# A chooser that also scores the last visit, and the denominators' step given out one visit sooner

## The chip, the cores and the metric

The kernel runs on one core of a Trainium2 chip. A core has five engines that run side by side and wait for each other through semaphores: PE (TensorE, matrix products into PSUM), DVE (VectorE), ACT (ScalarE), POOL (GpSimd) and SP (SyncE, which here issues the transfers). PSUM has eight banks; a bank holds a product until DVE or ACT has read it. The metric is the device time of one execution in microseconds (us). Before the change it is 592.06 us, the median of 3 runs (591.94 to 592.22).

## The reference

Two stages follow each other: attention through 32 induced points, for each of four images of 12480 rows of 128 channels, and a dense layer with a leaky activation.

```python
def mab(q, kv):
    s = scale * (q @ kv.transpose(0, 2, 1))
    s = s - s.max(-1, keepdims=True)
    a = np.exp(s)
    a /= a.sum(-1, keepdims=True) + 1e-09
    return a @ kv
h = mab(I, x)            # 32 induced points look at an image's rows
attn = mab(x, h)         # the rows look at the 32 results
...
h = x @ w_in             # 49920 rows, 128 -> 2048
g = np.maximum(h, 0.0) + alpha * np.minimum(h, 0.0)
out = g @ w_out          # 2048 -> 128
```

## The kernel before

**The dense layer carries the time.** The rows are worked in 98 blocks of up to four tiles of 128 rows. A block is gone through in *visits*, four for a block of four tiles and two for the very last block, which has two tiles: 390 visits, counted from 0. A visit (`visit`, L791) makes four first-stage products (L809: 128 of the 2048 features by up to 512 rows, each into a PSUM bank of its own, named `hh`) and four activations, each of which reads one bank and writes one second-stage operand, `gt`, to SBUF; ACT (L822) or DVE (L824) does each. The second stage (`second`, L827; products at L835) multiplies the four gts with the output weights and adds them in the block's PSUM bank `bp`. The leaky part is linear and is added by `linear` (L847, L862). Below, gt 156.2 is operand 2 of the operands 0 to 3 of visit 156, hh 156.2 the product it is made from; "aavv" means that ACT makes operands 0 and 1 of a visit and DVE 2 and 3.

**The order of PE** is: the products of visit n, then the second stage of visit n - 1, then the small products of the steps given out at visit n. PE works its queue in that order, so a first-stage product whose bank isn't free yet holds up the second stage behind it.

**The attention is woven in.** While one image is in the dense layer, the next image's induced points are worked out in small steps, given out at set visits with `at(n, fn, ..., cost=...)`. The steps at the end of an image's first attention, for images 1 to 3 (image 0 is done before the visits begin), are `a_max`, `a_factors`, `a_parts`, `a_den`, `a_sum` and `a_w_both`. `a_parts` (L557) joins the induced points' denominators: ACT makes the weights of the parts, `ex` (`a_worth`, L544), DVE multiplies them with the parts' sums, `ex` (`a_total`, L554), and adds these up, `den` (L555). `a_den`, two visits later, has PE turn `den` into the divisors (L568). The results are the same whenever between the last part and `a_den` this is done.

**Who does what is chosen by a model.** The class `Plan` keeps, for each of some 64 candidate plans, when PE, ACT and DVE will be free and when each bank will be. `choose` (L230) goes visit by visit: for each candidate it tries every split of the four activations, who does a block's copy out of PSUM (`finish`, L873: ACT at L888 or DVE at L890), and whether a step is done at once ("n") or held ("l"). A held step is run in the next visit, between operands 1 and 2 (`run_waiting`, called in `visit` when r is 2). `step` (L154) gives the state after the visit; its first entry is PE's time, which is nearly all of the score by which candidates are kept. The second stage that it counts in visit n is that of visit n - 1. In `step`, the parts of a step that is done at once follow each other, a DVE part starting when the ACT part is done (`busy[k] = ready = max(busy[k], ready) + ns`); a held step's parts are put on their engines one by one:

```python
if r == 2:
    for k, ns, ready, bank in late:
        busy[k] = max(busy[k], ready) + ns
```

The `ready` there is the one noted when the step was held, so a held DVE part doesn't wait in the model for the ACT part ahead of it. `plan.bank()` hands out the banks as the model chose them.

Of the kernel before, what the change touches and what calls it, by code (L numbers as in the profile page):

```python
# [30 lines left out]
def kernel(  # L31
# [80 lines left out]
    class Plan:  # L112
# [117 lines left out]
        def choose(self):  # L230
            start = tuple(430.0 if k == BANKS - 1 else 0.0 for k in range(BANKS))
            beam = [((0.0, 0.0, 330.0, (0.0,) * R, start, (), ()), None)]
            relus = ["".join(w) for w in product("av", repeat=R) if 0 < w.count("a") < R]
            for n, (*_, chains) in enumerate(self.visits):
                ways = []
                for chain in chains:
                    kinds = [k for k, _ in chain]
                    if "f" in kinds:
                        ways.append([e + w for e in "av" for w in "nl"])
                    elif "!" in kinds or not {"a", "v"} & set(kinds):  # L240
                        ways.append([""])
                    else:
                        ways.append(["n", "l"])
                found = {}
                for state, path in beam:
                    for way in product(*ways):
                        for relu in relus:
                            new, used = self.step(state, n, relu, way)
                            at = new[0] + 390
                            over = max(new[1] - at, 0) + max(new[2] - at, 0)  # L250
                            over += sum(w[1] for w in new[6]) * 0.3
                            score = new[0] + 0.3 * over
                            ends = sorted(max(x - new[0], -200) for x in new[4])
                            key = (
                                *(int(x - new[0]) // 16 for x in new[1:3] + new[3]),
                                *(int(x) // 16 for x in ends if x < self.NEVER / 2),
                                new[6],
                            )
                            if key not in found or score < found[key][0]:
                                found[key] = (score, new, (path, relu + "".join(way), used))  # L260
                best = sorted(found.values(), key=lambda f: f[0])[: self.WIDTH]
                beam = [(new, path) for _, new, path in best]
            path, taken, banks = beam[0][1], [], []
            while path:
                path, these, used = path
                taken.append(these)
                banks.append(used)
            self.taken = iter("".join(reversed(taken)))
            self.banks = iter([k for used in reversed(banks) for k in used])

    plan = Plan()
# [919 lines left out]
    visits = [(blk, i) for blk in blocks for i in range(NV // blk.per)]  # L1191
# [8 lines left out]
    def at(n, fn, *args, cost=()):  # L1200


        todo.setdefault(max(n, 0), []).append((fn, args, cost))
# [12 lines left out]
    for b, s, nt in groups[1:]:  # L1216
        n = first[b, s]
# [3 lines left out]
        if (b, s) == (0, 2):  # L1221
# [7 lines left out]
            cost=[("a", 100 + 27 * nt)],  # L1229
# [24 lines left out]
    for b in range(B - 1):  # L1254
        n = first[b, 0] - 1
        if b:
            at(n - 4, lambda b=b: states.__setitem__(b + 1, new_state(b + 1)))
        for p, pc in enumerate(whole_pieces):
            m = n + (8 * (p - 1 + (not b and p > 2)) if p > 1 else p)
            load, cast, turn = m - 3, m + 6, m + 8  # L1260
            score = m + 15 if p > 1 else n + 16
            look = score + 1 + (p == 1)
            join = m + (24 if p == whole_pieces[-1].k else 23) if p > 1 else n + (31 if p else 23)
            if not b:
                load, cast, turn = {
                    0: (-1, -1, 6), 1: (-1, 9, 10), 2: (4, 9, 11)
                }.get(p, (load, cast, turn))
                score, look = (score, look) if p > 1 else (score + 4, look + 4)
                join = n + 31 if p < 2 else n + 39 if p < 3 else join
            f = pc.full  # L1270
            if load >= 0:
                at(load, on, b + 1, a_load, pc)
            if cast >= 0:
                at(cast, on, b + 1, a_cast, pc)
            else:
                for q, v in enumerate((3, 4, 5, 5)):
                    at(v, on, b + 1, a_cast_act, pc, q * BT, BT, cost=[("a", 560)])
            at(turn, on, b + 1, a_turn, pc)
            small_at(
                score,  # L1280
                on,
                b + 1,
                a_scores_least,
                pc,
                cost=[("s", 215 if f else 85), ("v", 800 if f else 460)],
            )
            at(look, on, b + 1, a_exp, pc, cost=[("a", 717 if f else 430)])
            at(look + 2, on, b + 1, a_fac, pc, cost=[("a", 220)] if p else [])
            at(look + 1, on, b + 1, a_e1, pc)
            small_at(  # L1290
                join, on, b + 1, a_h_add, pc, cost=[("s", 226 if f else 115), ("v", 260)]
            )
        m = n + 8 * (NS - 2 + (not b)) + 15
        at(m + 2, on, b + 1, a_max, cost=[("a", 200)])
        at(m + 4, on, b + 1, a_factors, cost=[("s", 200), ("v", 170), ("a", 205)])
        at(m + 6, on, b + 1, a_parts, cost=[("a", 220), ("v", 260)])
        at(m + 8, on, b + 1, a_den, cost=[("s", 200), ("v", 370)])
        at(m + (12 if b else 10), on, b + 1, a_sum, cost=[("s", 200), ("v", 110)])
        small_at(m + 14, on, b + 1, a_w_both, cost=[("s", 220), ("a", 487)])
        small_at(m + 14, on, b + 1, a_lin, cost=[("s", 75), ("v", 190)])  # L1300
# [4 lines left out]
    for n, (blk, i) in enumerate(visits):  # L1305
        before = visits[n - 1][0] if n else None
        nt = before.nt * before.per if n else 0
        chains = [cost for _, _, cost in todo.get(n, ()) if cost]
        if i == 0 and n > NV:
            copy = ("f", 0) if n > ST else ("v", 610)  # L1310
            chains.insert(0, [("acc", before.k), copy])
            if n == 2 * NV:
                chains.insert(0, [("acc", 0), copy])
        both = [b.k for b in pairs.get(n, ())]
        cost = nt * Plan.FREE if both else 0
        plan.visits.append(
            (blk.nt * blk.per * P, cost, (both, [before.k] if n else []), nt, chains)
        )
    plan.choose()

    prev = None
# [49 lines left out]
```

## Time and profile before

| | |
|---|---|
| median of 3 runs | 592.06 us (591.94 to 592.22) |
| the profiled execution | 592.11 us, span 590.3 us |
| PE busy | 582.9 us, 99% |
| DVE busy | 535.0 us, 91% |
| ACT busy | 537.6 us, 91% |
| POOL busy | 217.1 us, 37% |
| first-stage products L809 on PE | 155.4 us, 1664 of them |
| second-stage products L835 on PE | 417.2 us, 6240 |
| activations on ACT, L822 | 455.3 us, 854 of 606 ns |
| activations on DVE, L824 | 453.7 us, 706 of 684 ns |

The span is the time from the first to the last instruction in the trace; the time of an execution has 1.8 us more around it. The page gives shares over the whole span. A line of the timeline is: start in us, length in us, engine, line of the kernel, operation, output and inputs, shapes, and "xN" where N such instructions follow each other (the length then runs from the first one's start to the last one's end, and instructions of one engine may overlap by a tenth of a microsecond); in brackets the idle time of the engine ahead of it and what ended that. A line of the list of waits is: the instruction that waited, what it waited for, the sum in us, how often, and the longest. A product's line on PE is its start; matrix products overlap, and the distance of two starts is what PE needs for one.

### The profile page before, as it was taken

How to read it: one execution, taken by the hardware profiler on the slowest of the kernel's cores; microseconds unless marked ns; L12 is line 12 of the kernel's file. 1: busy time of each engine (PE TensorE's matmuls, PEld its weight loads, DVE VectorE, ACT ScalarE, POOL GpSimd, SP SyncE). 2: the span in 40 equal slices, each digit the busy share in tenths (PEclk: the TensorE clock that was granted, in tenths of full speed). 3: DMA queues.
4: the chain of work that ended last, by engine and by line, in shares of the span. 5: the costliest groups of instructions: out<-in, count | busy, mean ns of one | idle time of the engine just before them, and what ended most of it. 6: DMA issues, size and time to landing. Idle time of an engine off the chain costs nothing.

```text
span 590.3 us, 23123 instructions
## 1 busy us (share of the span) xinstructions
PE 582.9 (99%) x9492; PEld 440.0 (75%) x9492; DVE 535.0 (91%) x979; ACT 537.6 (91%) x1087; POOL 217.1 (37%) x262
## 2 busy tenths in 40 slices
PE   9999999999999999999999999999999999999997
PEld 6577777777777777777777777777777777777776
DVE  5899999988998999999999899999999999999996
ACT  5799999999999999999999999999998998999986
POOL 3485552523325525413326256124034134144110
PEclk9999999999999999999999999999999999999999
DMA  8968699532188999332258899531331341433421
GB/s 336 276 181 176 158 250 197 132 98 73 39 240 159 209 216 222 94 95 58 78 152 181 194 255 204 136 100 38 92 77 50 92 81 49 118 85 57 92 69 47
DMA packets 122411, 80.56 MB, mean 136 GB/s; under 512 B 103824, under 2 KB 106176, under 8 KB 119232
## 3 DMA queue, kind: packets, MB, share of 16 engines
q1 hardware_dynamic: 122080, 78.99, 55.3%
q8 instruction: 74, 1.21, 0.8%
q14 instruction: 33, 0.27, 0.2%
q10 hardware_dynamic: 224, 0.09, 0.1%
HBM read 28.07 MB, written 25.56 MB: 91 GB/s over the span
## 4 chain that ended last, share of the span: by engine, by line
PE 95%; DMA 3%; DVE 1%; DVEq 0%; ACT 0%; issue 0%; POOL 0%; SPq 0%
PE bp L835 66%; PE hh L809 22%; DMA xs<-in_x_dram 3%; PE bp L862 2%; PE hh L645 2%; PE hh L473 1%; PE hh L379 1%; PE bp L960 0%; PE hh L364 0%; PE hh L599 0%; DVEq L1366 0%; PE hh L456 0%; DVE xn L349 0%; PE hh L583 0%; DVE hs L489 0%
## 5 line engine op out<-in xcount | busy, mean ns | idle before, releaser
L822 ACT ACTIVATE gt<-hh 128x512 bf16<-128x512 f32 x854 | 455.3, 606 | 34.4 <-PE hh L809 29.5
L824 DVE TENSOR_SCALAR gt<-hh 128x512 bf16<-128x512 f32 x706 | 453.7, 684 | 24.0 <-PE hh L809 13.6
L835 PE MATMUL bp<-W,gt 128*128 128x128 bf16 x6240 | 417.2, 220 | 0.7 <-DVE gt L824 0.7
L835 PEld LDWEIGHTS <-gt 128*128 128x128 bf16 x6240 | 349.4, 98 | 84.6 <-issue 76.0
L809 PE MATMUL hh<-a,HW 32*128 32x512 bf16 (+2 forms) x1664 | 155.4, 370 | 0.0
L759 POOL TENSOR_TENSOR rep<-e,rc 128x2048 bf16<-128x2048 f32 (+2 forms) x26 | 84.8, 3265 | 23.0 <-DVE rc L750 22.6
L727 POOL TENSOR_TENSOR e<-e,smx 128x512 f32<-128x512 f32 (+1 forms) x24 | 24.6, 1026 | 154.7 <-ACT gt L822 83.5
L809 PEld LDWEIGHTS <-HW 32*128 32x128 bf16 x1664 | 40.4, 91 | 41.6 <-issue 5.8
L713 POOL TENSOR_TENSOR t<-e 128x256 f32<-128x256 f32 (+1 forms) x24 | 17.2, 718 | 142.5 <-ACT e L689 142.5
L888 ACT COPY ob<-bp 128x512 f32<-128x512 f32 (+1 forms) x63 | 36.9, 586 | 4.5 <-PE bp L835 1.4
L713 POOL TENSOR_TENSOR t<-t 128x128 f32<-128x128 f32 (+3 forms) x100 | 30.5, 305 | 7.8
L330 POOL CAST xn<-xs 128x2048 bf16<-128x2048 f32 x17 | 32.1, 1890 | 0.8 <-DMA xs<-in_x_dram 0.3
L890 DVE COPY ob<-bp 128x512 f32<-128x512 f32 x31 | 21.3, 686 | 5.2 <-PE bp L835 5.2
L393 DVE TENSOR_SCALAR_CACHE_REDUCE s<-hh 128x512 f32<-128x512 f32 (+2 forms) x29 | 18.0, 619 | 1.6 <-PE hh L379 1.6
L862 PEld LDWEIGHTS <-a 32*128 32x128 bf16 x392 | 15.0, 93 | 5.7
L862 PE MATMUL bp<-HA,a 32*128 32x128 bf16 x392 | 19.1, 214 | 0.0
L418 ACT ACTIVATE e1T<-s,rm 128x512 bf16<-128x512 f32 (+1 forms) x25 | 18.0, 719 | 0.3
L722 DVE TENSOR_REDUCE smx<-e 128x16 f32<-128x512 f32 (+1 forms) x24 | 15.9, 662 | 0.0
L689 ACT ACTIVATE e<-e 128x512 f32<-128x512 f32 (+1 forms) x24 | 15.0, 624 | 0.0
L960 PE MATMUL bp<-blank 128*128 128x256 bf16 x78 | 13.6, 308 | 1.2 <-DVE blank L910 1.2
L489 DVE SCALAR_TENSOR_TENSOR hs<-hs,fac,hh 128x128 f32<-128x128 f32 (+1 forms) x25 | 8.6, 344 | 5.9 <-PE hh L473 5.2
L703 ACT COPY e<-hh 128x512 f32<-128x512 f32 (+1 forms) x22 | 13.4, 609 | 0.0
(107 smaller groups left out, 202.1 us busy)
## 6 DMA issues: line engine op xcount, KB each, us to landing
out_dram<-ob SPq DMA_DIRECT2D x97, 256.0 KB, 2.6
xs<-in_x_dram SPq DMA_DIRECT2D x23, 1024.0 KB, 6.1
xs<-in_x_dram SPq DMA_DIRECT2D x2, 512.0 KB, 9.2
w_in_f<-in_moe_w_in_dram SPq DMA_DIRECT2D x1, 1024.0 KB, 4.8
a<-rep SPq DMA_TRANSPOSE x27, 4.6
xT<-xn SPq DMA_TRANSPOSE x18, 5.7
e<-e1T SPq DMA_TRANSPOSE x18, 3.6
xs_left<-in_x_dram SPq DMA_DIRECT2D x4, 64.0 KB, 5.0
```

What stands on the lines that cost most here:

```text
L330: nc.gpsimd.tensor_copy(out=st.xn[s][:], in_=xs[:])
L393: nc.vector.tensor_scalar(out=s1[:parts, :cols], in0=ps[:parts, :cols], scalar1=-scale, scalar2=None, op0=MULT, op1=MIN, accum_out=st.mx[: ...
L713: nc.gpsimd.tensor_tensor(out=t[:, :n], in0=src[:, :n, :w], in1=src[:, :n, w : 2 * w], op=ADD)
L727: nc.gpsimd.tensor_tensor(out=st.e2[s][:, :n], in0=st.e2[s][:, :n], in1=st.m2[s][:, :n].unsqueeze(2).broadcast_to([P, n, M]), op=SUB,)
L759: nc.gpsimd.tensor_tensor(out=st.rep[s][:, ts], in0=st.e2[s][:, ts].unsqueeze(2).broadcast_to([P, n, R, M]), in1=rc[:, ts].unsqueeze(2).un ...
L809: nc.tensor.matmul(hh[:, q * cols + w.start : q * cols + w.stop], HWs[b][rows, v * P : (v + 1) * P], a2[rows, t0 : t0 + nt, :].rearrange(" ...
L822: nc.scalar.activation(out=gt[:, :cols], in_=hh[:, :cols], func=RELU)
L824: nc.vector.tensor_relu(gt[:, :cols], hh[:, :cols])
L835: nc.tensor.matmul(blk.acc[:, t * C : (t + 1) * C], gt[:, (q * nt + t) * P : (q * nt + t + 1) * P], W1[:, k, :], start=(not blk.begun), st ...
L862: nc.tensor.matmul(blk.acc[w, t * C : (t + 1) * C], blk.a2[rows, blk.t0 + t, w], HAs[b][rows, :], start=(not blk.begun and t == 0), stop=F ...
L888: nc.scalar.copy(out=ob[:, :nt], in_=acc)
L890: nc.vector.tensor_copy(out=ob[:, :nt], in_=acc)
```

## The change

Two edits. The chooser's score for the last visit (n = 389) is replaced: instead of PE's time with some weight on how late ACT and DVE are, it is the time at which the second stage of this visit itself would end, operand by operand, each taken when PE is free and the operand is ready. `plan.end` is the number of products that an operand takes there, 4. And `a_parts` is given out at m + 5 in place of m + 6, for each of images 1 to 3.

```diff
                             score = new[0] + 0.3 * over
+                            if n == len(self.visits) - 1:
+                                score = new[0] - self.MODE
+                                for ready in new[3]:
+                                    score = max(score, ready + self.SEM) + self.end * self.FREE
                             ends = sorted(max(x - new[0], -200) for x in new[4])
...
         at(m + 4, on, b + 1, a_factors, cost=[("s", 200), ("v", 170), ("a", 205)])
-        at(m + 6, on, b + 1, a_parts, cost=[("a", 220), ("v", 260)])
+        at(m + 5, on, b + 1, a_parts, cost=[("a", 220), ("v", 260)])
         at(m + 8, on, b + 1, a_den, cost=[("s", 200), ("v", 370)])
...
+    plan.end = visits[-1][0].nt * visits[-1][0].per
     plan.choose()
```

What becomes of it in the built program: PE, POOL and SP have the same instructions in the same order. On ACT and DVE the order differs at four places, and the rest is the same:

```
image 1, visits 68 and 69
  ACT before  gt68.0 gt68.1 gt69.0 gt69.1 [ex] gt69.3 gt70.0 gt70.1
  ACT after   gt68.0 gt68.1 [ex] [copy ob] gt69.2 gt69.3 gt70.0 gt70.1 gt70.2
  DVE before  gt67.3 gt68.2 gt68.3 [copy ob] [ex den] gt69.2 [rc] gt70.2 gt70.3
  DVE after   gt67.3 [ex den] gt68.2 gt68.3 gt69.0 gt69.1 [rc] gt70.3
image 2, visit 156 (image 3, visit 252, likewise)
  ACT both    gt156.0 gt156.1 [ex] [copy ob] gt157.2 gt157.3
  DVE before  gt155.3 gt156.2 gt156.3 [ex den] gt157.0 gt157.1
  DVE after   gt155.3 [ex den] gt156.2 gt156.3 gt157.0 gt157.1
the last two visits
  ACT before  gt388.0 gt388.1 [copy ob] gt389.2 gt389.3 [copy ob, last]
  ACT after   gt388.0 gt388.1 gt388.2 gt389.0 gt389.1 [copy ob] [copy ob, last]
  DVE before  gt388.2 gt388.3 gt389.0 gt389.1
  DVE after   gt388.3 gt389.2 gt389.3
```

For images 2 and 3 `a_parts` was done at once, in visits 156 and 252; now it is given out in visits 155 and 251 and held. For image 1 it was held before, too. In visits 70 to 192 many products get another bank number, and so does hh 389.3. These bank pairings are the same before and after: hh 157.3 is written to the bank that gt 156.2 empties, hh 253.3 to that of gt 252.2, and hh 69.2 to that of gt 68.2.

## The prediction

> **What bounds the kernel now.** I read the page first (busy shares, granted clock, chain), then the list of waits, then the timeline at the places where the order of instructions moves. Products and their operands are named as in the section on the kernel: gt 156.2 is the third of the four second-stage operands of visit 156 (counted from 0), hh 157.3 the fourth first-stage product of visit 157.
>
> ```profile
> span 590.3 us, 23123 instructions
> ...
> PE 582.9 (99%) x9492; PEld 440.0 (75%) x9492; DVE 535.0 (91%) x979; ACT 537.6 (91%) x1087; POOL 217.1 (37%) x262
> ...
> PEclk9999999999999999999999999999999999999999
> ...
> PE 95%; DMA 3%; DVE 1%; DVEq 0%; ACT 0%; issue 0%; POOL 0%; SPq 0%
> ```
>
> PE is the bound: busy 99% at full granted clock, 95% of the chain. DVE and ACT, at 91%, are close behind. So a moved DVE or ACT instruction costs nothing while PE finds its operands and its PSUM banks ready, and costs one for one as soon as it doesn't: PE has no idle time in which to catch up. The list of waits says how often that happens now:
>
> ```profile
> DVE ex L554 <- ACT ex L544: 1.0, 1, 1.0
> ...
> PE bp L835 <- DVE gt L824: 0.7, 2, 0.5
> ```
>
> PE waits for an operand twice, for 0.7 us in all, and DVE waits for ACT's `ex` once. All three belong to places that the change touches: 0.49 and 0.95 us at `a_parts` of image 1 (timeline at 132 to 133 us), 0.20 us in the very last visit (585.66).
>
> **The change, part by part.** PE, GpSimd and SP get the same instructions in the same order as before, so no product, transfer or GpSimd step is added or dropped, and no queue of those three is passed. On DVE and ACT the four activations' split differs in visits 69, 70, 388 and 389, one `ob` copy goes from DVE to ACT, and `a_parts` (ACT `ex`, then DVE `ex` and `den`) stands earlier for images 1 to 3.
>
> *Images 2 and 3.* For image 2 the DVE pair `ex`, `den` used to stand behind gt 156.3 and now stands ahead of gt 156.2. ACT's `ex` doesn't move: on its queue it follows gt 156.1 in both. The timeline of before, DVE, ACT and PE:
>
> ```profile
> 256.70 0.69 DVE L824 TENSOR_SCALAR gt<-hh 128x512 bf16<-128x512 f32 x1
> ...
> 257.66 0.30 ACT L544 ACTIVATE ex<-rm 128x7 f32<-128x7 f32 x1
> 257.75 0.40 PE L809 MATMUL hh<-a,HW 32*128 32x512 bf16 x4
> ...
> 257.99 0.17 DVE L554 TENSOR_TENSOR ex<-ex,da 128x7 f32<-128x7 f32 x1
> 258.08 1.07 PE L835 MATMUL bp<-W,gt 128*128 128x128 bf16 x16
> ...
> 258.27 0.68 DVE L824 TENSOR_SCALAR gt<-hh 128x512 bf16<-128x512 f32 x1
> ...
> 258.87 0.68 DVE L824 TENSOR_SCALAR gt<-hh 128x512 bf16<-128x512 f32 x1
> ```
>
> ACT's `ex` ends at 257.66 + 0.30 = 257.96, and DVE's `ex` already starts 0.03 us behind it. It can't start sooner after the change. So DVE stands still with both gts of visit 156 queued behind the wait, and the place at 258.27, which was gt 157.0's, becomes that of gt 156.2: it ends at 258.27 + 0.68 = 258.95 instead of 256.70 + 0.69 = 257.39.
>
> Who waits for it: hh 157.3, because in both kernels it is written to the PSUM bank that gt 156.2 empties. It was started at 257.75, with 0.36 us to spare; now it can't before 258.95 plus the time from a DVE end to PE's start. For that the trace has one row pair, in image 1 below (DVE ends at 132.31 + 0.68 = 132.99, PE goes on at 133.05: 0.06 us); I take 0.06, with ends at 0 and at 0.20 (the whole idle time of the last visit). PE's next work, the second-stage products of visit 156, starts 258.08 - 257.75 = 0.33 us behind: 258.95 + 0.06 + 0.33 = 259.34 instead of 258.08, **+1.26 us**. Nothing is added to it after that: a product takes 1.00 / 16 = 0.0625 us, so gt 156.3 (end 258.87 + 0.68 = 259.55) is wanted at 259.34 + 12 x 0.0625 = 260.09; gt 157.0 and 157.1, two steps of 0.60 us later (260.15 and 260.75), are wanted at 260.66 and 260.91. That is a margin of 0.10 us for the last, so a second wait is near. DVE is level with PE again at gt 158.1.
>
> Image 3 has the same order and the same bank pairing (hh 253.3 behind gt 252.2):
>
> ```profile
> 395.57 0.30 ACT L544 ACTIVATE ex<-rm 128x7 f32<-128x7 f32 x1
> ...
> 395.66 0.39 PE L809 MATMUL hh<-a,HW 32*128 32x512 bf16 x4
> ...
> 395.98 1.07 PE L835 MATMUL bp<-W,gt 128*128 128x128 bf16 x16
> ...
> 396.18 1.96 DVE L824 TENSOR_SCALAR gt<-hh 128x512 bf16<-128x512 f32 x3
> ```
>
> 396.18 + 0.68 + 0.06 + 0.32 = 397.24 instead of 395.98: **+1.26 us**.
>
> *Image 1.* Here the triple moves by a whole visit, from between gt 69.1 and 69.2 to between gt 68.1 and 68.2; the copy of L890 leaves DVE for ACT, and visit 69 becomes DVE, DVE, ACT, ACT.
>
> ```profile
> 129.66 1.08 ACT L822 ACTIVATE gt<-hh 128x512 bf16<-128x512 f32 x2
> 130.25 0.43 PE L809 MATMUL hh<-a,HW 32*128 32x512 bf16 x4
> 130.40 0.68 DVE L890 COPY ob<-bp 128x512 f32<-128x512 f32 x1
> 130.61 1.07 PE L835 MATMUL bp<-W,gt 128*128 128x128 bf16 x16
> ...
> 131.70 0.30 ACT L544 ACTIVATE ex<-rm 128x7 f32<-128x7 f32 x1
> ...
> 131.93 0.62 PE L835 MATMUL bp<-W,gt 128*128 128x128 bf16 x8
> 132.03 0.17 DVE L554 TENSOR_TENSOR ex<-ex,da 128x7 f32<-128x7 f32 x1 [0.95 <-ACT ex L544]
> ...
> 132.31 0.68 DVE L824 TENSOR_SCALAR gt<-hh 128x512 bf16<-128x512 f32 x1
> ...
> 133.05 0.62 PE L835 MATMUL bp<-W,gt 128*128 128x128 bf16 x8 [0.49 <-DVE gt L824]
> 133.50 0.36 PE L568 MATMUL hh<-mf,den 128*128 128x32 f32 x2
> ```
>
> Before, PE stops in the middle of visit 69's second stage: eight products from 131.93, then the ninth at 133.05 instead of 131.93 + 8 x 0.0625 = 132.43. These **0.62 us are gained back**. But a longer stop comes one visit earlier. ACT's two gts of visit 68 (129.66, 1.08 long) end at 130.74; `ex` overlaps the one ahead of it by 0.12 (130.73 + 1.09 against 131.70 in the old place) and ends near 130.92. DVE's `ex` follows at 130.95, gt 68.2 another 132.31 - 132.03 = 0.28 later at 131.23, ending at 131.91. hh 69.2 is written to the bank that gt 68.2 empties, so it starts at 131.97 and not at 130.25, and visit 68's second stage at 131.97 + 0.32 = 132.29 instead of 130.61: +1.68. Net of the old stop: **+1.06 us**. The copy on ACT lies behind this stop (its next gt waits for hh 69.2 anyway) and costs nothing; without that cover it would cost the 0.6 us of an ACT copy. `rc` of L750 comes some 0.7 us later, and the 3.6 us GpSimd product behind it has several visits until its transposed result is read: nothing.
>
> *The other banks.* From visit 70 to 192 the same tiles get other bank numbers, mostly a plain renaming. PE's first-stage products show no idle time before, so no gain is to be had; the cost is between 0 and one wait like the 0.49 above. I take 0.
>
> *The last visit.* It is scored by what its own second stage costs.
>
> ```profile
> 583.77 0.41 PE L809 MATMUL hh<-a,HW 32*128 32x64 bf16 x32
> 583.88 0.59 ACT L888 COPY ob<-bp 128x512 f32<-128x512 f32 x1 [0.34 <-PE bp L835]
> ...
> 584.12 1.34 PE L835 MATMUL bp<-W,gt 128*128 128x128 bf16 x20
> 584.31 1.29 DVE L824 TENSOR_SCALAR gt<-hh 128x512 bf16<-128x512 f32 x2 [0.43 <-PE hh L809]
> 584.36 1.09 ACT L822 ACTIVATE gt<-hh 128x512 bf16<-128x512 f32 x2
> 584.49 0.38 SPq L898 DMA_DIRECT2D out_dram<-ob  x1
> 585.66 0.84 PE L835 MATMUL bp<-W,gt 128*128 128x128 bf16 x12 [0.20 <-DVE gt L824]
> ```
>
> PE reads the operands in order 0 to 3. Before, DVE makes 0 and 1, one behind the other, and PE waits for 1 (584.31 + 1.29 = 585.60) until 585.66. After, ACT makes 0 and 1, DVE 2 and 3, and the copy is held back behind ACT's pair (its old place at 583.88 goes to the gt that ACT takes over in visit 388). ACT can start when DVE did, at 584.31; its pair, 1.09 long, ends at 585.40, so PE goes on at 585.46: **-0.20 us**. Operand 3 (DVE, 585.60) is wanted at 585.46 + 0.50. The held copy ends near 585.9, and its transfer is issued 1.4 us later than at 584.49, still ahead of the last two, which follow the copy behind PE's end. The ends of this term are -0.29 (PE without any wait: 584.12 + 20 x 0.0625 = 585.37 against 585.66) and 0 (the last transfers caught behind that one).
>
> **The sum**: 1.06 + 1.26 + 1.26 - 0.20 = **+3.38 us**. The profiled execution took 592.11 us (span 590.3 and 1.8 around it), the median is 592.06: 595.4 us from either. What a measurement of this kernel can tell from no change is about 0.2%, 1.2 us.
>
> [...] In the trace the granted clock holds through the stop of image 1:
>
> ```profile
> 131.60:133.10 1.50, 1.01 (x15) 0.61 (x14) 1.03 (x5) 1.50 (x5) 0.64 (x3) 1.00 0.46 175
> 133.10:137.10 4.00, 4.00 (x72) 3.24 (x72) 3.68 (x9) 3.09 (x7) 3.61 (x1) 1.00 0.00 0
> ```
>
> The clock column is 1.00 in and behind a stop of 0.5 us; no stop of 1.7 us is in this trace. [...]
>
> **The rivals.**
> 1. *Not slower*: gt 156.2 and its twins have enough slack that DVE's wait is hidden, image 1's stop goes, and the end is shorter: 592.06 - 0.62 - 0.20 = 591.2. For it: both of PE's old waits go, and DVE is idle for 9% of the span. Against it: the place is the bank of hh 157.3, the price 1.26 us, and it decides as soon as gt 156.2 ends later than 257.75 - 0.06; the rows put it at 258.95. 4%.
> 2. *Only images 2 and 3 pay*: in image 1 the old stop goes and the new one is hidden, since the copy has left DVE: 592.06 + 2.52 - 0.62 - 0.20 = 593.8. Against it: ACT's `ex` can't end before 130.9, whatever DVE has to do. 8%.
> 3. *Knock-on*: the 0.10 us margin at gt 157.1 (and its like in the other two images) fails, or a renumbered bank waits; a wait of 0.49 in each image: 595.4 + 1.5 = 596.9. 9%.
> 4. [...] 2%.
> 5. *The change does nothing that shows* (DVE's `ex` doesn't hold the gts): 592. Against it: the 0.95 us in image 1, where gt 69.2 stood behind exactly this wait while its product was done by 130.7. 1%.
>
> **How the numbers follow.** The forecast, 595.4, has 76%; its own range, from the ends above (three times -0.06 to +0.14, the last visit -0.09 to +0.20), is 595.1 to 596.1. Reaching to rival 2 below and most of the way to rival 3 above gives 593.7 to 596.6, which leaves out less than 2 in 10. Faster by over 0.2% needs 590.9 or less, below even rival 1: 1%. Within 0.2%: rivals 1 and 5, 5%. Slower: 94%.
>
> **What the next profile would show.** DVE `ex` L554 waiting for ACT `ex` L544 three times, some 1.3 us in images 2 and 3 and 1.8 in image 1; PE idle ahead of L809 for DVE gt, 1.2 to 1.7 us each; no wait of L835 at visit 69; the last L835 wait down to some 0.1 us or none. The prediction falls if PE shows no wait at L809 near 131.9, 258.9 and 398 us, or if waits of the same size stand anywhere else.

## The result, and the profile after

The changed kernel takes 595.89 us (median of 6 runs, 595.51 to 596.17) against 592.06 us of the kernel before (median of 6 on the same chip, 591.92 to 592.58): a ratio of 1.0062 (95% interval 1.0051 to 1.0073), 3.83 us more. 595.4 was forecast. The profiled execution took 595.51 us, 0.38 below the median, with a span of 593.7. The page of the changed kernel, first the shares and the granted clock, then the chain, then two groups of PE (busy us, mean ns, idle us just before them):

```profile
span 593.7 us, 23121 instructions
PE 584.5 (98%) x9492; PEld 440.5 (74%) x9492; DVE 533.1 (90%) x977; ACT 538.6 (91%) x1089; POOL 217.0 (37%) x262
...
PEclk9999999999999999999999999999999999999999
...
PE 93%; DMA 3%; DVE 2%; ACT 1%; issue 0%; POOL 0%; ACTq 0%; DVEq 0%; SPq 0%
...
L839 PE MATMUL bp<-W,gt 128*128 128x128 bf16 x6240 | 417.1, 220 | 0.1
...
L813 PE MATMUL hh<-a,HW 32*128 32x512 bf16 (+2 forms) x1664 | 156.9, 370 | 3.1 <-DVE gt L828 3.1
```

Line numbers are 4 higher than before (L813 is the first-stage product, L839 the second-stage one, L828 DVE's gt, L558 DVE's `ex`, L548 ACT's). The second-stage products are as busy as before (417.1 and 417.2 us). New are the 3.1 us of idle time ahead of first-stage products, all of them for a gt of DVE, and DVE's share of the chain, 2% instead of 1%. The list of waits has the cause and the effect, three times each, and has lost PE's 0.7 us at L835:

```profile
DVE ex L558 <- ACT ex L548: 4.5, 3, 1.8
...
PE hh L813 <- DVE gt L828: 3.1, 3, 1.3
```

The timeline of the changed kernel at image 2, where the prediction's arithmetic was longest:

```profile
258.84 0.30 ACT L548 ACTIVATE ex<-rm 128x7 f32<-128x7 f32 x1
258.93 0.39 PE L813 MATMUL hh<-a,HW 32*128 32x512 bf16 x3
259.03 0.59 ACT L892 COPY ob<-bp 128x512 f32<-128x512 f32 x1
259.17 0.17 DVE L558 TENSOR_TENSOR ex<-ex,da 128x7 f32<-128x7 f32 x1 [1.35 <-ACT ex L548]
...
259.45 2.47 DVE L828 TENSOR_SCALAR gt<-hh 128x512 bf16<-128x512 f32 x4
...
260.18 0.37 PE L813 MATMUL hh<-a,HW 32*128 32x512 bf16 x1 [0.86 <-DVE gt L828]
260.49 1.07 PE L839 MATMUL bp<-W,gt 128*128 128x128 bf16 x16
```

DVE stands for 1.35 us behind ACT's `ex`, which ends at 258.84 + 0.30 = 259.14. Then it makes gt 156.2, 156.3, 157.0 and 157.1 in one piece. Three of visit 157's four first-stage products start from 258.93 on, the fourth, hh 157.3, waits until 260.18, and with it the whole second stage of visit 156, which starts 1.56 us behind 258.93 instead of 0.33. So the loss is 1.23 us, though the bracket shows 0.86: an idle time is counted from the recorded end of the last product, not from where the next could have started. Image 3 is the same (DVE waits 1.35 us, PE 0.86, at 398 and 399 us).

Image 1 in the changed kernel:

```profile
130.00 0.39 PE L813 MATMUL hh<-a,HW 32*128 32x512 bf16 x2
...
130.37 0.32 ACT L548 ACTIVATE ex<-rm 128x7 f32<-128x7 f32 x1
...
130.71 0.17 DVE L558 TENSOR_TENSOR ex<-ex,da 128x7 f32<-128x7 f32 x1 [1.80 <-ACT ex L548]
...
130.99 2.47 DVE L828 TENSOR_SCALAR gt<-hh 128x512 bf16<-128x512 f32 x4
...
131.73 0.39 PE L813 MATMUL hh<-a,HW 32*128 32x512 bf16 x2 [1.33 <-DVE gt L828]
132.05 1.07 PE L839 MATMUL bp<-W,gt 128*128 128x128 bf16 x16
...
133.38 1.07 PE L839 MATMUL bp<-W,gt 128*128 128x128 bf16 x16
```

PE stops at hh 69.2 for DVE's gt 68.2, and in visit 69 the sixteen second-stage products (133.38) run in one piece where before they came eight and eight with the stop between. The end of the program:

```profile
587.75 2.17 PE L839 MATMUL bp<-W,gt 128*128 128x128 bf16 x32
587.94 1.08 ACT L826 ACTIVATE gt<-hh 128x512 bf16<-128x512 f32 x2 [0.27 <-PE hh L813]
587.95 1.29 DVE L828 TENSOR_SCALAR gt<-hh 128x512 bf16<-128x512 f32 x2 [0.99 <-PE hh L813]
588.91 0.59 ACT L892 COPY ob<-bp 128x512 f32<-128x512 f32 x1
...
589.53 0.38 SPq L902 DMA_DIRECT2D out_dram<-ob  x1
```

The last 32 products run without a stop.

**Where the time went.** The start of each visit's first product in the changed kernel, less that in the kernel before, tells where PE falls behind. It changes at six places only: by +1.68 at visit 70 and -0.67 at 71 (image 1, +1.02 net), +0.10 at visit 101 and +0.31 at 135, +1.23 at 158 (image 2), +1.23 at 254 (image 3), and -0.24 at the end. That is 1.02 + 0.40 + 1.23 + 1.23 - 0.24 = +3.64 us. The stretch ahead of the visits differs by -0.25 between these two executions; in all the profiles shown here it lies between -0.43 and +0.44 of the kernel before, whatever was changed, so it belongs to no edit. So the spans of these two executions differ by 3.4, while the medians, each over executions whose first stretch may differ likewise, differ by 3.83.

The steps at visits 101 and 135 weren't in the forecast. This is the first of them:

```profile
174.07 0.40 PE L813 MATMUL hh<-a,HW 32*128 32x512 bf16 x4
174.92 1.29 DVE L828 TENSOR_SCALAR gt<-hh 128x512 bf16<-128x512 f32 x2 [0.39 <-ACT e L693]
175.40 0.63 PE L813 MATMUL hh<-a,HW 32*128 32x512 bf16 x4
```

DVE's gt 99.0 could be made once its product is done (174.07 + some 0.4) but starts at 174.92, 0.35 us later than the like instruction of other visits, and the next visit's four first-stage products take 0.63 us instead of 0.40: the fourth of them starts at 175.66, 0.05 behind the end of gt 99.0 (175.61), which frees a bank. The release named in the bracket is only the nearest event. The second case is gt 133.0 at 224.20.

### The profile page after: what moved, and what is told of

It is laid out like the page before. It is cut to its first block, busy times and chain, and to the rows that moved or that the text cites. A ratio compares the mean times of both kernels' runs of the same rounds, so it can differ in the third digit from the quotient of the medians.

```text
span 593.7 us, 23121 instructions
## 1 busy us (share of the span) xinstructions
PE 584.5 (98%) x9492; PEld 440.5 (74%) x9492; DVE 533.1 (90%) x977; ACT 538.6 (91%) x1089; POOL 217.0 (37%) x262
## 4 chain that ended last, share of the span: by engine, by line
PE 93%; DMA 3%; DVE 2%; ACT 1%; issue 0%; POOL 0%; ACTq 0%; DVEq 0%; SPq 0%
PE bp L839 64%; PE hh L813 21%; DMA xs<-in_x_dram 3%; PE bp L866 2%; PE hh L649 2%; PE hh L477 1%; DVE gt L828 1%; PE hh L383 1%; ACT gt L826 1%; PE bp L964 0%; PE hh L368 0%; PE hh L603 0%; DVE hs L493 0%; PE hh L460 0%; DVE xn L353 0%
## 5 line engine op out<-in xcount | busy, mean ns | idle before, releaser
L828 DVE TENSOR_SCALAR gt<-hh 128x512 bf16<-128x512 f32 x705 | 452.5, 683 | 25.3 <-PE hh L813 13.9
L839 PE MATMUL bp<-W,gt 128*128 128x128 bf16 x6240 | 417.1, 220 | 0.1
L839 PEld LDWEIGHTS <-gt 128*128 128x128 bf16 x6240 | 349.3, 98 | 86.5 <-issue 78.7
L813 PE MATMUL hh<-a,HW 32*128 32x512 bf16 (+2 forms) x1664 | 156.9, 370 | 3.1 <-DVE gt L828 3.1
L731 POOL TENSOR_TENSOR e<-e,smx 128x512 f32<-128x512 f32 (+1 forms) x24 | 24.6, 1026 | 157.1 <-ACT gt L826 79.4
L813 PEld LDWEIGHTS <-HW 32*128 32x128 bf16 x1664 | 40.5, 91 | 43.2 <-issue 7.4
L892 ACT COPY ob<-bp 128x512 f32<-128x512 f32 x64 | 37.5, 586 | 3.6 <-PE bp L839 0.7
(107 smaller groups left out, 202.0 us busy)
```

The source lines that it names most:

```text
L731: nc.gpsimd.tensor_tensor(out=st.e2[s][:, :n], in0=st.e2[s][:, :n], in1=st.m2[s][:, :n].unsqueeze(2).broadcast_to([P, n, M]), op=SUB,)
L813: nc.tensor.matmul(hh[:, q * cols + w.start : q * cols + w.stop], HWs[b][rows, v * P : (v + 1) * P], a2[rows, t0 : t0 + nt, :].rearrange(" ...
L828: nc.vector.tensor_relu(gt[:, :cols], hh[:, :cols])
L839: nc.tensor.matmul(blk.acc[:, t * C : (t + 1) * C], gt[:, (q * nt + t) * P : (q * nt + t + 1) * P], W1[:, k, :], start=(not blk.begun), st ...
L892: nc.scalar.copy(out=ob[:, :nt], in_=acc)
```

## The experiments

The changed kernel makes two edits, and the second acts at three images. The theory ("queue theory" in the expectations) is the prediction's: a held `a_parts` puts DVE's `ex` ahead of two gts, it waits there for ACT's `ex`, and PE loses what the gts come late. The table gives, for each kernel, by how much PE fell behind the kernel before in stretches of visits (the differences of start times at visits 65, 80, 150, 165, 248, 262 and 389, one profile each, us), their sum, and the median less that of the kernel before on the same chip, which was 592.06 to 592.23. A positive number is time lost. What happens between the first visit and visit 65 isn't in the table; it is nothing but for +0.12 in the kernel before with one less on DVE and +0.10 in the last kernel, both taken up below:

| kernel | image 1 (65-80) | 80-150 | image 2 (150-165) | 165-248 | image 3 (248-262) | 262-389 | end | sum | median |
|---|---|---|---|---|---|---|---|---|---|
| the change | +1.02 | +0.40 | +1.23 | 0 | +1.23 | 0 | -0.24 | +3.64 | +3.83 |
| score alone | 0 | 0 | 0 | 0 | 0 | 0 | -0.19 | -0.19 | -0.22 |
| step moved, old score | +1.02 | +0.41 | +1.23 | 0 | +1.23 | 0 | +0.01 | +3.90 | +4.05 |
| moved for images 2, 3 | 0 | 0 | +1.23 | +0.28 | +1.23 | 0 | -0.25 | +2.49 | +2.11 |
| moved for image 1 | +1.02 | +0.42 | 0 | 0 | 0 | 0 | -0.25 | +1.19 | +1.16 |
| model mended | -0.48 | +0.14 | +0.02 | +0.32 | -0.26 | +0.26 | -0.21 | -0.21 | -0.22 |
| step split | -0.25 | +0.42 | 0 | 0 | 0 | 0 | -0.22 | -0.05 | -0.27 |
| model mended, m + 6 | -0.52 | 0 | 0 | 0 | 0 | +0.09 | -0.23 | -0.66 | -0.90 |
| other banks | +0.94 | +0.41 | +1.18 | -0.01 | +1.18 | 0 | -0.22 | +3.48 | +3.33 |
| one more on DVE | +1.02 | 0 | +1.23 | +0.80 | +1.23 | 0 | -0.25 | +4.03 | +3.46 |
| before, one less on DVE | 0 | +0.40 | -0.01 | 0 | -0.28 | 0 | +0.01 | +0.12 | +0.11 |
| model mended, m + 6, spares 7 and 6 | -0.54 | -0.01 | -0.01 | 0 | -0.28 | +0.26 | -0.24 | -0.83 | -0.81 |
| model mended, m + 6, spares 2 and 3 | -0.54 | +0.37 | -0.01 | 0 | -0.28 | +0.11 | -0.25 | -0.61 | -0.59 |

**Each edit alone.** First the score without the move:

```diff
-        at(m + 5, on, b + 1, a_parts, cost=[("a", 220), ("v", 260)])
+        at(m + 6, on, b + 1, a_parts, cost=[("a", 220), ("v", 260)])
```

> The new score of the last visit alone, a_parts back at m + 6. Queue theory (the cost of the change is DVE's ex and den waiting for ACT's ex with gts queued behind them): only the last two visits differ from before, the last second stage loses most of its 0.36 us wait: 592.06 - 0.24 = 591.8, and no late DVE start in visits 99 and 133. Rival (the new score costs, by a worse plan somewhere): over 592.6.

Measured: 591.93 us (591.51 to 593.75), ratio 0.9999 (0.999 to 1.0008). The end is 0.19 us shorter and no other place moves. That is too little for a median to tell; the place shows it. Then the move without the score:

```diff
-                            if n == len(self.visits) - 1:
-                                score = new[0] - self.MODE
-                                for ready in new[3]:
-                                    score = max(score, ready + self.SEM) + self.end * self.FREE
...
-    plan.end = visits[-1][0].nt * visits[-1][0].per
```

> a_parts at m + 5 alone, with the old score. Queue theory: everything of the changed kernel but the gain at the end: 595.9 + 0.24 = 596.1, three waits of DVE's ex for ACT's ex, 4.5 us in all. Rival (score and step only cost together): under 593. If the two late DVE starts (gt 99.0 and gt 133.0, about 0.35 us each) belong to the new bank numbers of visits 70 to 192, they are there again; if they are chance, not at both of these places.

Measured: 596.20 us (595.5 to 596.48), ratio 1.0061 (1.0048 to 1.0074). Every step of the whole change is there but the one at the end. So all of the loss belongs to the moved step, and the two edits don't act on each other.

**Each image alone.** Images 2 and 3:

```diff
-        at(m + 5, on, b + 1, a_parts, cost=[("a", 220), ("v", 260)])
+        at(m + (5 if b else 6), on, b + 1, a_parts, cost=[("a", 220), ("v", 260)])
```

> a_parts at m + 5 for images 2 and 3 only, m + 6 for image 1; new score. The bank numbers of visits 70 to 192 are those of before. Queue theory: 592.06 + 2 x 1.23 - 0.24 = 594.3, PE's first-stage products wait 1.25 us for DVE gt twice, the old stop of 0.66 us in visit 69 is still there. Rival (image 1 carries the loss): 592 to 593. Rival (the renumbered banks carry much of it): the same 594.3, but then the next run has over 593.5.

Measured: 594.26 us (594.0 to 594.39), ratio 1.0032 (1.002 to 1.0044). And image 1:

```diff
-        at(m + 5, on, b + 1, a_parts, cost=[("a", 220), ("v", 260)])
+        at(m + (6 if b else 5), on, b + 1, a_parts, cost=[("a", 220), ("v", 260)])
```

> a_parts at m + 5 for image 1 only; new score. Queue theory: 592.06 + 1.02 - 0.24 = 592.8, and 0.40 more, 593.2, if the late DVE starts in visits 99 and 133 come with the new bank numbers, which this kernel has too. Rival (image 1's old stop goes and the new one is hidden): 591.2.

Measured: 593.31 us (592.98 to 595.05), ratio 1.002 (1.0011 to 1.0028). The waits of the kernel with images 2 and 3 moved, then of that with image 1 moved:

```profile
DVE ex L558 <- ACT ex L548: 3.6, 3, 1.3
...
PE hh L813 <- DVE gt L828: 1.7, 2, 0.9
```

```profile
DVE ex L558 <- ACT ex L548: 1.8, 1, 1.8
...
PE hh L813 <- DVE gt L828: 1.3, 1, 1.3
```

With images 2 and 3 the three waits are those two and the old one of image 1 (3.6 us in all against 4.5). The two kernels are 2.11 and 1.16 us over the kernel before, 3.27 together. Both have the gain of 0.24 at the end, which the whole change has once, so by these medians the change should cost 3.27 + 0.24 = 3.51, 0.32 less than it does. The places are the firmer evidence: each image's step is the same alone as together. The late DVE starts come with image 1's edit and not with those of images 2 and 3.

**The same step, with a model that knows the wait.** If DVE's standing behind ACT's `ex` is the cause, a chooser that counts it should put the step elsewhere:

```diff
-                    for k, ns, ready, bank in late:
-                        busy[k] = max(busy[k], ready) + ns
+                    done = 0
+                    for k, ns, ready, bank, linked in late:
+                        ready = max(ready, done) if linked else ready
+                        busy[k] = done = max(busy[k], ready) + ns
...
-                ready, bank = 0, None
+                ready, bank, held_one = 0, None, False
...
-                        waits.append((k, ns, ready, bank))
+                        waits.append((k, ns, ready, bank, held_one))
+                        held_one = True
```

> The changed kernel with the chooser's model mended: a held step's DVE part waits for the held ACT part ahead of it. The plan then has ACT make ex ahead of its gts and DVE take gt n.0 and n.1 before ex and den, so DVE has nothing to wait for. Queue theory: the three new stops and the old one of 0.66 us are gone, the end stays shorter: 592.06 - 0.67 - 0.24 = 591.15, or 591.5 if the new bank numbers bring late DVE starts again. Rival (the place one visit sooner costs whatever the order, since two more instructions stand ahead of the gts): 594 to 595.

Measured: 592.01 us (591.56 to 592.56), ratio 0.9991 (0.9979 to 1.0004). Given out at m + 5 as in the change, the step costs nothing: image 1 gains 0.48, images 2 and 3 are where they were. By the kinds of instructions (which operand a gt makes may differ), the order of ACT and DVE is that of the changed kernel but at the three images: there ACT's `ex` stands two gts sooner and DVE's `ex` and `den` two gts later. The timeline of that kernel at image 2 shows why; ACT's `ex` is done 1.01 us before DVE comes to its own:

```profile
255.77 0.36 ACT L551 ACTIVATE ex<-rm 128x7 f32<-128x7 f32 x1
...
257.14 0.16 DVE L561 TENSOR_TENSOR ex<-ex,da 128x7 f32<-128x7 f32 x1
```

I had expected 591.15 to 591.5; what is missing went to late starts of the kind shown above at two other instructions (+0.31 at visit 204 behind gt 202.0, +0.25 at 275) and to a step of +0.14 at visit 116. That step is likely of the same kind on ACT, though no run tests it: ACT's five gts from 191.35 on take 2.69 us here and 2.56 in the kernel with the mended model at m + 6 below, and one of the five is number 576 of ACT's records, a place of the sort that the late starts turn out to have. The -0.26 at image 3 is one that the kernel before has there and this one hasn't.

**The two halves of the step a visit apart.** ACT's part at m + 5, DVE's at m + 6:

```diff
-        at(m + 5, on, b + 1, a_parts, cost=[("a", 220), ("v", 260)])
+        at(m + 5, on, b + 1, lambda st: plan.then(lambda: a_worth(st)), cost=[("a", 220)])
+        at(m + 6, on, b + 1, lambda st: plan.then(lambda: a_total(st)), cost=[("v", 260)])
```

> Only ACT's part of a_parts goes out at m + 5, DVE's part stays at m + 6; new score, model as it was. Queue theory: for images 2 and 3 the order is that of before; for image 1 ACT's ex ends near 130.9 and DVE's ex follows gt 68.3 with a wait of some 0.5 us that the slack of gt 69.0 covers, so the old stop goes: 591.2, or 591.6 with the late DVE starts in visits 99 and 133. Rival (the sooner ACT part is what costs): over 593.

Measured: 591.96 us (591.68 to 592.83), ratio 0.9998 (0.999 to 1.0007). By the kinds of instructions, ACT's order is that of the changed kernel, and DVE's differs in one thing: at each image `ex` and `den` stand two gts later. Of the three waits of DVE one of 0.5 us is left, and the list has no wait of PE's in the dense layer:

```profile
DVE gt L828 <- ACT ob L892: 0.6, 1, 0.6
...
DVE ex L558 <- ACT ex L548: 0.5, 1, 0.5
```

So it isn't the earlier visit of ACT's half that costs, but that DVE's half goes into it as well, ahead of two gts. The first of these lines is one of the late starts: they are here too, and take back 0.42 of what image 1 and the end gain. I had expected 591.6 with them. Image 1 gains only 0.25 of the 0.67: four of its first-stage products, from 131.21 on, take 0.74 us where those of the kernel before (131.61) take 0.40. What holds them up wasn't looked at.

**The mended model with the step at its old visit.** The edit above and `m + 6`:

> The mended model and the new score with a_parts at m + 6 as before. In image 1 the copy and ex change places on ACT and DVE takes gt 69.0 and 69.1 before ex. Queue theory: 592.06 - 0.67 - 0.24 = 591.15, or 591.6 with the late DVE starts. Same banks as in the split kernel, so these two should have the same time within 0.2 us. Rival: image 1's old stop had another cause than DVE's wait and is still there: 591.8.

Measured: 591.33 us (591.03 to 591.92; before 592.23), ratio 0.9986 (0.9977 to 0.9995). It is the best of all, 0.9 us below the kernel before on the same chip: a small gain, but one that the interval excludes from being none. Its page, then its timeline at image 1:

```profile
span 589.2 us, 23123 instructions
...
L842 PE MATMUL bp<-W,gt 128*128 128x128 bf16 x6240 | 417.0, 220 | 0.1
...
L816 PE MATMUL hh<-a,HW 32*128 32x512 bf16 (+2 forms) x1664 | 155.6, 370 | 0.0
```

```profile
130.66 0.34 ACT L551 ACTIVATE ex<-rm 128x7 f32<-128x7 f32 x1
...
131.53 0.19 DVE L561 TENSOR_TENSOR ex<-ex,da 128x7 f32<-128x7 f32 x1
```

The time lies between the two that were expected (591.15, or 591.6 with late starts), but not within 0.2 us of the split kernel, which is 0.63 slower: that one has the late starts at visits 101 and 135, +0.42, and gains 0.27 less at image 1. PE's idle time ahead of L816 is zero, and DVE's `ex` starts 0.53 us behind the end of ACT's without a wait. The old stop of image 1 is gone and no new one has come.

**Is the bank the cause, or the late gts?** In the prediction hh 157.3 waits since it gets the bank of gt 156.2. Here the three products get banks that ACT empties:

```diff
-            self.banks = iter([k for used in reversed(banks) for k in used])
+            names, out = list(range(BANKS)), []
+            other = {(69, 2): (68, 1), (157, 3): (156, 1), (253, 3): (252, 1)}
+            banks.reverse()
+            for n, used in enumerate(banks):
+                for r, k in enumerate(used):
+                    if (n, r) in other:
+                        v, q = other[n, r]
+                        j = banks[v][q]
+                        names[k], names[j] = names[j], names[k]
+                    out.append(names[k])
+            self.banks = iter(out)
```

> The changed kernel with the bank pairing taken away: hh 69.2, hh 157.3 and hh 253.3 get the bank that ACT's gt 68.1, 156.1 and 252.1 empties, the engines' orders stay. Bank rival (the stop is the bank wait itself, and the operands would still be in time): 3 x 1.2 us come back, 592.3. Queue theory (gt n.2 and n.3 are late whatever the bank): PE stops some 0.4 us twice in the second stage of visits 68, 156 and 252 and 0.3 us in the next one, 1.0 to 1.2 us per image: 595.7 to 595.9, with the waits at the second-stage products and not at the first-stage ones.

Measured: 595.56 us (595.28 to 597.26), ratio 1.0062 (1.0049 to 1.0074), the same as the change. The list of waits and the timeline at image 2 of this kernel (L849 is the second stage, L838 DVE's gt):

```profile
DVE ex L568 <- ACT ex L558: 4.5, 3, 1.8
...
PE bp L849 <- DVE gt L838: 1.4, 6, 0.3
```

```profile
260.27 0.40 PE L849 MATMUL bp<-W,gt 128*128 128x128 bf16 x4 [0.26 <-DVE gt L838]
...
260.87 0.40 PE L849 MATMUL bp<-W,gt 128*128 128x128 bf16 x4 [0.20 <-DVE gt L838]
```

The time is a little below the 595.7 to 595.9 that were expected. No first-stage product waits for a gt of DVE any more (one in image 1 waits 0.15 us for a gt of ACT), and images 2 and 3 still cost 1.18 us each instead of 1.23: PE gets to the second stage sooner and stops there, between the operands, for the same gts. The bank only says where PE shows the loss; the root is DVE's 1.35 us.

**The late starts of DVE.** My first theory for them, that they come with the bank numbers that the change renames, fell with the split step and the mended model at m + 6: those two have the same banks and the same splits, and only the first starts gt 99.0 and gt 133.0 late. What the profiles with late starts share is the place of these two instructions in DVE's stream: counting its records in the trace, semaphore instructions too, they are numbers 448 and 576; where they start in time, they have other numbers. So the place was moved alone, by one spare instruction at the start of the changed kernel:

```diff
+    spare = const.tile([P, 1], f32, name="spare")
+    nc.vector.memset(spare[:], 0.0)
```

> The changed kernel with one more DVE instruction, a memset of one column that nobody reads, among the memsets at the start; every other instruction, split and bank as in the changed kernel. Place theory (the late DVE starts of gt 99.0 and gt 133.0 belong to the place of these instructions in DVE's stream, 433 and 557 instructions from its start in all five kernels that have them, 434 and more in the five that don't): both are gone, 0.40 us less, 595.5. Bank theory (they come with the new bank numbers): both are there, 595.9.

and, in the kernel before, by one instruction less (its memset goes to GpSimd):

```diff
-    for t in (xn_left, blank, e1T_left):
+    for t in (xn_left, blank):
         nc.vector.memset(t[:], 0.0)
...
+    nc.gpsimd.memset(e1T_left[:], 0.0)
```

> The kernel before with one DVE instruction less: the memset of e1T_left goes to GpSimd; all else as before. Place theory: gt 99.0 and gt 133.0 move to places 433 and 557 and start some 0.35 us late, PE loses 0.4 us: 592.06 + 0.40 = 592.5. Bank theory: nothing, 592.1.

Measured: 595.61 us (594.81 to 596.25) for the first, ratio 1.0056 (1.0043 to 1.0068), and 592.26 us (591.91 to 593.91) for the second, ratio 1.0006 (0.9997 to 1.0015). Neither median tells 0.4 us from nothing; the profiles do. With the spare instruction the steps at visits 101 and 135 are gone, and DVE makes five gts in one piece where gt 99.0 stood alone; with one less on DVE, in the kernel before, whose profile has neither, they appear, +0.10 and +0.31, at the same two instructions. (592.5 was expected there; PE also gains 0.28 at visit 249, which comes next, and loses 0.12 at visit 32, where ACT's number 192, a gt at 73.86, starts late.) The timeline of DVE, first with the spare instruction, then with one less:

```profile
172.87 3.33 DVE L828 TENSOR_SCALAR gt<-hh 128x512 bf16<-128x512 f32 x5
```

```profile
173.83 1.29 DVE L824 TENSOR_SCALAR gt<-hh 128x512 bf16<-128x512 f32 x2 [0.40 <-ACT e L689]
```

The same is seen on ACT, unsought. The kernel before has a gt (247.0) whose idle time is 0.64 us, its number on ACT 1216; in the kernel with one less on DVE ACT happens to have one instruction more ahead of it, and there the idle time is 0.36 us and PE gains 0.28 us at visit 249. Before, then the kernel with one less on DVE:

```profile
387.38 2.55 ACT L822 ACTIVATE gt<-hh 128x512 bf16<-128x512 f32 x5 [0.64 <-PE hh L809]
```

```profile
387.18 2.56 ACT L822 ACTIVATE gt<-hh 128x512 bf16<-128x512 f32 x5 [0.36 <-PE hh L809]
```

**Foretelling the late starts.** The numbers 448, 576 and 1216 are 64 plus 3, 4 and 9 times 128. That gives a rule which can be tested by counting, so two kernels were made from the best one, the mended model at m + 6, with spare instructions at the start chosen from its trace: seven on DVE and six on ACT, so that nearly all of the numbers 64 + k x 128 fall on instructions that wait for their own engine anyway, and two and three, so that they fall on four instructions that had never been late.

```diff
+    spare = const.tile([P, 7], f32, name="spare")
+    for i in range(7):
+        nc.vector.memset(spare[:, i : i + 1], 0.0)
...
+    spare_a = const.tile([P, 6], f32, name="spare_a")
+    for i in range(6):
+        nc.scalar.copy(out=spare_a[:, i : i + 1], in_=spare[:, :1])
```

> This is the mended model with the step at m + 6, with seven spare memsets on DVE and six spare copies on ACT at the very start. Block theory: in all twelve profiles so far, counting every record of DVE or of ACT in the trace, semaphore instructions too, an instruction that follows a semaphore instruction and has nothing else to wait for starts 42 to 47 ns after it, and 321 to 413 ns after it where its number is 64 + a multiple of 128. So the late starts can be foretold by counting. Shifted by seven and six, the numbers 64 + k x 128 fall on instructions that are held up by their engine's own work by 450 ns or more anyway, but for one: no late start on ACT, and on DVE a single one, near 565 us. Then PE gains what the mended model gained (0.52 at image 1, 0.23 at the end) and the 0.28 us that ACT's late start costs at visit 249, and doesn't lose the 0.09 at visit 310; it may lose up to 0.3 near 565 us: 0.75 to 1.05 us less than before, 591.0 to 591.3. Rival, place by place: that the late starts come at certain instructions for reasons of their own. Then ACT's at 346 and 386 us stay, and the time is 591.3 as without the spares.

> The same kernel with two spare memsets on DVE and three spare copies on ACT. Block theory: late starts (idle 0.3 us or more behind a wait that had passed) of DVE near 70.8 and 220.6 us and of ACT near 191.3 and 542.2 us, at instructions that started in time in every kernel so far, and none at those of the kernel without the spares (DVE near 273.6 and 472.2, ACT near 346.6 and 386.4). PE loses 0 to 0.3 at each of the four and gains the 0.28 at visit 249: 590.9 to 592.0. Rival, place by place: late starts where they are without the spares, 591.3.

Measured: 591.41 us (591.05 to 593.29; before 592.22), ratio 0.9991 (0.9982 to 1.0), and 591.63 us (591.29 to 592.48), ratio 0.9992 (0.9984 to 1.0001). All places came as foretold: with seven and six one late start, on DVE, and none on ACT; with two and three the four named and no other. The first kernel's time lies 0.11 above the expected 591.0 to 591.3; against the kernel before on its chip it is 0.81 less, where 0.75 to 1.05 less were expected. The second's lies inside its range. The one on DVE in the first kernel, then one of ACT's in the second, whose idle time without the spares is 0.15 us:

```profile
565.97 2.49 DVE L831 TENSOR_SCALAR gt<-hh 128x512 bf16<-128x512 f32 x4 [0.46 <-PE hh L816]
```

```profile
192.19 2.06 ACT L829 ACTIVATE gt<-hh 128x512 bf16<-128x512 f32 x4 [0.43 <-PE hh L816]
```

PE gained the 0.28 at visit 249 in both. What the late starts cost it was at the upper end of what I expected in the first (0.26 near 565 us) and in the middle in the second (0.6 for the four, of which 0.1 at visit 30). Neither median is below that of the kernel without the spares (591.33). By the places the first gains 0.17 more than that kernel, too little for the medians to show; the second gains 0.05 less, and 0.15 with visit 30: what shifting takes away at one place it gives back at another.

Left open is a wait of first-stage products for a transfer at visit 240, 0.8 us in the profile of the kernel with one spare instruction and 0.3 in that with images 2 and 3 moved, and in no other. It is the +0.80 and the +0.28 of the table. In both kernels the sum is above the median's difference (4.03 against 3.46, 2.49 against 2.11), so it may not come in every execution; its cause wasn't looked for.

## Why the prediction was right

The time, 595.89 us, is 0.5 above the forecast and inside its own range; the mechanism is the one named, at the places named. Point by point:

- *Images 2 and 3, +1.26 each.* Measured +1.23 each, together and alone. DVE waits 1.35 us behind `ex` and PE at the product named. The chain of arithmetic held to 0.03 us, since each of its terms was the length of the same instruction in the trace of the kernel before. The 0.10 us margin at gt 157.1 held, too: no second wait.
- *Image 1, +1.06.* Measured +1.02: the new stop +1.68 (+1.68), the old one gone -0.67 (-0.62).
- *The last visit, -0.20.* Measured -0.24, and -0.19 to -0.25 in the other kernels with the new score, inside the ends.
- *"The other banks ... I take 0".* This is the term that was mis-sized: +0.40 between visits 80 and 150, inside the range from 0 to 0.49 that stood beside it. That it fell inside is luck, since the range was made for a wait for a bank, and it isn't the banks: the changed kernel with one spare instruction has the same banks and loses nothing there. It comes from two gts, numbers 448 and 576 of DVE's records, that start about 0.35 us late behind a wait; image 1's edit moved them to these places. Without it PE's loss would have been 3.24 us.
- *The signs.* DVE's `ex` waits 1.35, 1.35 and 1.80 us (1.3 and 1.8 were named), the wait of the second stage at visit 69 and the last one are gone, and no new wait of that size stands elsewhere. One sign was misjudged: PE's idle time ahead of the first-stage products was to be 1.2 to 1.7 us each, and the brackets show 0.86, 1.33 and 0.86. The loss is as foretold; the bracket counts only from the recorded end of the product before.
- *Rival 1, not slower*, asked for slack at gt 156.2; the 1.35 us went to PE but for 0.12. *Rival 2*, image 1's stop hidden: it is 1.68. *Rival 3*, a wait of 0.49 in each image: there are none behind the stops, and the 0.40 that did come lies elsewhere and has another cause. *Rival 5*, no effect: against three waits of 4.5 us.
- *Rival 4, the clock drops.* The windows of the changed kernel with the stop of image 1 and behind it (the column behind POOL's is the granted clock):

```profile
130.30:132.00 1.70, 0.37 (x4) 0.09 (x1) 1.25 (x4) 0.86 (x3) 1.30 (x6) 1.00 0.00 0
132.00:136.00 4.00, 4.00 (x68) 3.25 (x70) 3.35 (x8) 3.56 (x7) 2.45 (x2) 1.00 0.17 66
```

The clock stays at 1.00 through a stop with 1.33 us of idle PE. No stop between products is longer than 1.42 us in any run here, but behind PE's last product the kernel before and the changed one have a longer idle time, 3.8 us to the end of the span, and there the granted clock does fall to 0.50: 2.6 us behind the product in the kernel before (windows 586.50 to 589.10 at 1.00, then 0.50) and 3.7 us behind it in the changed one (589.93 to 593.65 at 1.00, then 0.50). So the prediction, for which no stop of 1.7 us was in its trace, overlooked that one. How long a stop between products can be before the clock falls isn't shown by any run.

What was also right is the reading of the chooser: in its model a held DVE part doesn't wait for the ACT part. The kernel with that mended is the direct test: the same step, given out at the same visit, costs nothing at images 2 and 3 instead of 1.23.

## What to carry to other kernels

A step of two engines that is given out sooner needn't be done sooner: its second half goes into the second engine's queue and holds all that is behind it until the first half, at its own place in the first engine's queue, is done; here DVE stood 1.35, 1.35 and 1.80 us for it. Before such a move, take the end of the first half from the trace and count what stands behind the second half; if a planner decides, check that its model chains the parts of a held step, since a chooser fills whatever gap its model doesn't see. With the new score, mending the model and leaving the step where it was gave 591.33 us, the score alone 591.93, each against a kernel before of 592.2 on its chip.

## What the runs showed of the hardware

**A late start every 128 instructions.** In the fourteen profiles (before, after and the twelve experiments) there are, behind the first 31 us, 2829 DVE and ACT instructions that follow a semaphore instruction which passed while the engine had nothing else to do. 2794 of them start at most 47 ns after it. The other 35 start 321 to 338 ns (ACT, 23) and 395 to 416 ns (DVE, 12) after it, and these are all of them, and only they, whose number among the engine's records is 64 + a multiple of 128. So where a semaphore instruction that had passed was number 63 + a multiple of 128 and the engine had nothing else to do, the instruction behind it lost about 0.28 us (ACT) or 0.35 us (DVE); where the engine was busy for longer than that anyway (0.45 us or more at all such places but one in the kernel with spares 7 and 6), nothing showed. PE lost up to 0.31 us for one, or nothing. The bracket of such a row names whatever event was nearest, not a release. What delays the start isn't shown: the runs changed only which instructions stand at these places.

So instructions added or dropped early in this kernel shifted which ones start late, and with that its time by some tenths of a us: in the changed kernel 0.40 us of the 3.64, in the kernel before with one less on DVE +0.12, +0.10 and +0.31 at three places and -0.28 at another. That is a floor under what a difference of 0.1% says about an edit of it.
